# Channel gate over a 384x384x384 image on one core: a shorter lead load with the weight on the same queue, and the first tile gated in two parts

## Chip, cores, metric

One NeuronCore of one Trainium2 chip. The metric is the device time of one execution in microseconds. A run counts as slow here when it is over 1.5% above the fastest of its kernel.

## The reference

```python
def reference(x, w1d):                      # x: (1, 384, 384, 384) bf16, w1d: (1,) bf16
    g = jnp.einsum("bhwc->bc", x) / (H * W) # mean of each channel over all pixels
    s = _sigmoid(g * w1d[0])                # cut: with k = 1 the padding and loop come to this
    return x * s[:, None, None, :]
```

The gate is the sigmoid that multiplies x, one value for each channel. It needs the mean over the whole image before the first output element is known, so a plain kernel reads x twice. At 113.25 MB for one pass over x, that would be three passes of traffic.

## The kernel before

The kernel guesses. A "row" here is 128 pixels times 384 channels, 98,304 bytes. It computes a sigmoid (`s_early`) from the first 4 rows, gates and stores every tile with it while the true sums go on, and compares the bf16 result with the true sigmoid at the end. Only if they differ does a second pass run (it doesn't with these inputs). So x is read once and the output written once.

Data come in a lead of 12 rows and 19 tiles of 60 rows, in four slots of SBUF, the on-chip memory. DVE is the vector engine. A packet is one piece that a DMA engine moves, as the trace records it; a load or store lands when its end is signalled. Loads go to SyncE's queue; of the first three tiles half goes to ScalarE's queue, which later carries all stores. TensorE sums 52 rows of each tile with matmuls against ones, DVE sums the other 8 and does the gating. The weight (2 bytes) was queued on ScalarE behind half of the first tile:

```python
FIRST, EARLY, TILE, SLOTS, BOTH, OWN, PAUSE = 12, 4, 60, 4, 3, 8, 8
...
    load(base, FIRST, 0)                                     # lead: 12 rows, SyncE
    for k in range(BOTH):
        load(slot(k), TILE, row0(k), ("sync", "scalar"))     # halves of 30 rows
        if k == 0:
            plan.dma("scalar", w_one[0:1, 0:1], w1d.unsqueeze(0), writes=["w_one"])
    for k in range(BOTH, SLOTS):
        load(slot(k), TILE, row0(k))
    weight()                     # one matmul that spreads the weight; TensorE's first
    sum_first()                  # 3 matmuls over 4 rows
    ...                          # s_early on ScalarE
        def one(e, s):           # TensorE, each tile: 39 matmuls, one signal at their end
            e.wait_ge(ready, 1).then_inc(ready, -1)
            add_rows(e, 1, slot(s) * C, TILE - OWN, False, False).then_inc(
                plan.sems["tensor"], 1
            )
    ...
    def put(place, n, r0, to=None):          # gate in place on DVE, then store
        plan.op("vector", gate(to, place, n, s_early), ...)
        plan.final.append(
            plan.dma("scalar", dram(o_rows, r0, n), at(to, n), reads=rows(to, n))
        )
    ...
    for k in range(n_tiles):
        if k >= SLOTS:
            for i in ...:        # cut: which tiles are put here
                sum_own(i)       # DVE's 8 rows of tile i
                put(slot(i), TILE, row0(i))
            if k == SLOTS:
                pause(slot(k))   # ScalarE: waits for the first store, then 8 rows of dummy work
            load(slot(k), TILE, row0(k), ...)   # waits for the store that frees the slot
```

The gate overwrites the tile in place, so it must wait until TensorE has summed it.

## Time and profile before

528.62 us, median of the first 3 runs (528.31 to 529.32).

The lines below are of the page of the kernel before: the span, busy time by engine, and, in 40 slices of the span, DVE's busy tenths, the DMA engines' busy tenths and the GB/s moved; then the DMA queues (q1 is SyncE's, q10 ScalarE's) with packets, megabytes and share of 16 engines' span.

```profile
span 527.0 us, 1015 instructions
PE 198.5 (38%) x754; PEld 0.2 (0%) x2; DVE 353.9 (67%) x81; ACT 5.5 (1%) x5; POOL 0.3 (0%) x5
...
DVE  0639999649494858576666666666666666758892
...
DMA  9999999999999999999999999999999999999998
GB/s 383 434 421 418 448 448 395 444 448 448 395 444 448 448 395 444 448 444 399 444 448 444 399 444 448 445 399 444 444 444 406 441 444 444 406 441 444 444 406 363
...
q10 hardware_dynamic: 3314, 122.10, 53.6%
q1 hardware_dynamic: 2880, 104.40, 46.1%
...
HBM read 113.25 MB, written 113.25 MB: 430 GB/s over the span
```

53.6% and 46.1% are 99.7%: the DMA engines are busy the whole time. DVE is next with 67%. The slices of 395 and 448 GB/s are an effect of which whole packets fall into a slice; longer windows show the rate. The next lines are from the windows view of the kernel before: stretch, its length, busy time (count) of PE, PEld, DVE, ACT and POOL, then TensorE's clock, the DMA engines' busy share and GB/s.

```profile
0.00:10.00 10.00, 0.00 (x0) 0.00 (x0) 0.17 (x1) 1.49 (x2) 0.30 (x5) 1.00 0.93 376
10.00:44.00 34.00, 20.10 (x75) 0.20 (x2) 16.52 (x10) 0.61 (x1) 0.00 (x0) 1.00 1.00 430
50.00:56.00 6.00, 5.06 (x24) 0.00 (x0) 5.97 (x3) 0.00 (x0) 0.00 (x0) 1.00 1.00 369
100.00:480.00 380.00, 143.99 (x546) 0.00 (x0) 249.30 (x43) 0.00 (x0) 0.00 (x0) 0.69 1.00 434
```

From 10 to 44 us there are only loads (430 GB/s), from 100 to 480 us loads and stores (434 GB/s). Two stretches are lower: the first 10 us and the 6 us around the first store.

The timeline of the kernel before, early stage (start, duration, engine, line, what; in brackets the engine's idle time before it and what ended it):

```profile
15.31 0.16 PE L409 MATMUL w_all<-w_one,ones 1*128 1x1 bf16 x1 [15.31 <-DMA w_one<-in_w1d_dram]
...
19.63 0.61 ACT L440 ACTIVATE s_early<-total,w_scaled 128x384 bf16<-128x384 f32 x1 [15.80 <-DVE total L315]
...
24.18 11.17 PE L244 MATMUL acc<-arena,ones 128*128 128x512 bf16 x39 [6.04 <-PEq L283]
35.45 12.16 DVE L207 TENSOR_TENSOR arena<-arena,s_early 128x23040 bf16<-128x23040 bf16 x1 [10.63 <-PE acc L244]
...
47.64 18.36 ACTq L109 DMA_DIRECT2D out_dram<-arena  x2
```

TensorE waits 15.31 us for the weight, the early sigmoid runs at 19.63, the first tile's sums start at 24.18 when its SyncE half has landed, DVE waits 10.63 us for the 39 matmuls, and the first store is issued at 47.64. The end, from the chain of waits of the kernel before (start, duration, what):

```profile
403.47 47.25 DMA out_dram<-arena
...
450.74 38.79 DMA arena<-in_x_dram
...
489.55 12.16 DVE arena L207
```

This chain names the things that ended last, but a link of it can be covered by queued DMA work. At 489.5 to 501.7 us, for example, DVE gates the last tile while the DMA engines still work off earlier stores.

### The profile page before, as it was taken

To read this page: it belongs to the slowest core of one execution; us is meant where nothing else is said; L and a number is where in the kernel's file an instruction comes from. 1 tells how busy PE (TensorE), PEld (TensorE's weight loads), DVE (VectorE), ACT (ScalarE), POOL (GpSimd) and SP (SyncE) were. 2 spreads that over 40 slices of the span, in tenths; PEclk is the share of its full clock that TensorE was granted. 3 is DMA by queue.
4 is the path that set the end of the run, shared out by engine and by line. 5 is a ranking of instruction groups with operands and counts; after the bars stand their busy time and mean duration, and the time that the engine had idled before them with its cause. 6 is when DMAs were issued, how large, how long until landed. Compare 5 with 4: busy or idle time off the path is not lost. (4 is left out here: it accounts for less than half of the span.)

```text
span 527.0 us, 1015 instructions
## 1 busy us (share of the span) xinstructions
PE 198.5 (38%) x754; PEld 0.2 (0%) x2; DVE 353.9 (67%) x81; ACT 5.5 (1%) x5; POOL 0.3 (0%) x5
## 2 busy tenths in 40 slices
PE   0389170070706151524333342516060707070810
PEld 0000000000000000000000000000000000000000
DVE  0639999649494858576666666666666666758892
ACT  1000020000000000000000000000000000000000
POOL 0000000000000000000000000000000000000000
PEclk9999766576767667675758585858585858585765
DMA  9999999999999999999999999999999999999998
GB/s 383 434 421 418 448 448 395 444 448 448 395 444 448 448 395 444 448 444 399 444 448 444 399 444 448 445 399 444 444 444 406 441 444 444 406 441 444 444 406 363
DMA packets 6196, 226.51 MB, mean 430 GB/s; under 512 B 690, under 2 KB 690, under 8 KB 690
## 3 DMA queue, kind: packets, MB, share of 16 engines
q10 hardware_dynamic: 3314, 122.10, 53.6%
q1 hardware_dynamic: 2880, 104.40, 46.1%
q14 instruction: 2, 0.02, 0.0%
HBM read 113.25 MB, written 113.25 MB: 430 GB/s over the span
## 5 line engine op out<-in xcount | busy, mean ns | idle before, releaser
L244 PE MATMUL acc<-arena,ones 128*128 128x512 bf16 x749 | 196.6, 429 | 288.4 <-PEq L283 288.4
L207 DVE TENSOR_TENSOR arena<-arena,s_early 128x23040 bf16<-128x23040 bf16 (+1 forms) x20 | 233.5, 11677 | 78.0 <-PE acc L244 73.6
L327 DVE TENSOR_REDUCE part<-arena 128x384 f32<-128x3072 bf16 x18 | 96.4, 5355 | 67.3 <-DMA arena<-in_x_dram 67.3
L334 DVE TENSOR_TENSOR own<-own,part 128x384 f32<-128x384 f32 x18 | 10.0, 558 | 0.6
L418 DVE TENSOR_SCALAR w_scaled<-w_all 128x1 f32<-128x1 f32 x2 | 0.2, 152 | 14.3 <-PE w_all L409 14.3
L409 PE MATMUL w_all<-w_one,ones 1*128 1x1 bf16 x1 | 0.2, 158 | 15.3 <-DMA w_one<-in_w1d_dram 15.3
L244 PE MATMUL acc_own<-terms,ones 128*128 128x384 bf16 x3 | 1.4, 479 | 10.5 <-DVE terms L345 10.5
L327 DVE TENSOR_REDUCE own<-arena 128x384 f32<-128x3072 bf16 x1 | 5.3, 5305 | 0.0
L474 ACT ACTIVATE arena<-total,w_scaled 128x384 bf16<-128x384 f32 x1 | 0.6, 615 | 439.0 <-DVE total L315 439.0
L315 DVE TENSOR_TENSOR total<-total,acc 128x128 f32<-128x128 f32 (+2 forms) x11 | 4.5, 408 | 0.4
L392 ACT ACTIVATE arena<-warm 128x3072 bf16<-128x3072 f32 x1 | 2.8, 2763 | 54.1 <-DMA out_dram<-arena 54.1
L313 DVE COPY total<-acc 128x384 f32<-128x384 f32 x1 | 0.6, 558 | 1.2 <-PE acc L244 1.2
L403 ACT ACT_TABLE_LOAD x1 | 1.3, 1283 | 2.3 <-issue 2.3
L352 DVE TENSOR_TENSOR own<-own,terms 128x384 f32<-128x384 f32 x2 | 1.1, 558 | 0.1
L345 DVE CAST terms<-own 128x384 bf16<-128x384 f32 x3 | 1.1, 357 | 0.1
L482 DVE TENSOR_TENSOR total<-arena,s_early 128x384 f32<-128x384 uint16 x1 | 0.6, 557 | 0.7 <-ACT arena L474 0.7
L370 DVE TENSOR_TENSOR total<-total,acc_own 128x384 f32<-128x384 f32 x1 | 0.6, 554 | 0.6 <-PE acc_own L244 0.6
L426 DVE MEMSET ones<- 128x128 bf16 x1 | 0.2, 165 | 1.0 <-PEq L596 1.0
L440 ACT ACTIVATE s_early<-total,w_scaled 128x384 bf16<-128x384 f32 x1 | 0.6, 615 | 15.8 <-DVE total L315 15.8
L242 PE MATMUL acc<-arena,ones 128*128 128x512 bf16 x1 | 0.6, 608 | 0.0
L490 DVE TENSOR_REDUCE wrong<-total 128x1 f32<-128x384 f32 x1 | 0.6, 552 | 0.0
L403 ACT ACTIVATE warm<-warm 128x1 f32<-128x1 f32 x1 | 0.2, 203 | 0.0
(8 smaller groups left out, 0.9 us busy)
## 6 DMA issues: line engine op xcount, KB each, us to landing
out_dram<-arena ACTq DMA_DIRECT2D x19, 5760.0 KB, 47.4
arena<-in_x_dram SPq DMA_DIRECT2D x16, 5760.0 KB, 38.9
arena<-in_x_dram ACTq DMA_DIRECT2D x3, 2880.0 KB, 27.4
arena<-in_x_dram SPq DMA_DIRECT2D x3, 2880.0 KB, 36.4
arena<-in_x_dram SPq DMA_DIRECT2D x1, 1152.0 KB, 10.3
out_dram<-arena ACTq DMA_DIRECT2D x1, 1152.0 KB, 16.9
w_one<-in_w1d_dram ACTq DMA_DIRECT2D x1, 0.0 KB
```

Source lines behind the costliest of these rows:

```text
L207: return lambda e: e.tensor_tensor(to_v, v, s_b, ALU.mult)
L242: loaded.append(e.matmul(bank, weights, moving, start=start, stop=stop))
L244: return e.add_instruction(mybir.InstMatmult(name=nc.get_next_instruction_name(), engine=mybir.EngineType.PE, ins=[e.lower_ap(moving), e.l ...
L313: emit = lambda e, part=part, of=of: e.tensor_copy(part, of)
L315: emit = lambda e, part=part, of=of: e.tensor_tensor(part, part, of, ALU.add)
L327: lambda e: e.reduce_sum(to[:], view, axis=mybir.AxisListType.X),
L334: lambda e: e.tensor_tensor(own[:], own[:], part[:], ALU.add),
L345: lambda e, term=term: e.tensor_copy(term, own[:]),
L352: lambda e, term=term: e.tensor_tensor(own[:], own[:], term, ALU.subtract),
L370: lambda e: e.tensor_tensor(total[:], total[:], acc_own[:, :C], ALU.add),
L392: lambda e: e.activation(to, warm[:, 0:1].broadcast_to([P, PAUSE * C]), ACT_F.Sigmoid),
L403: lambda e: e.activation(warm[:, 1:2], warm[:, 0:1], ACT_F.Sigmoid),
```

## The change

Its intent: get the early sigmoid, the first gate and so the first store sooner. The lead shrinks to 8 rows with the weight right behind it on SyncE; the other 4 rows go to ScalarE's queue behind its half of the first tile; TensorE signals after 32 of the 52 rows of a tile, and the first tile is gated in parts of 32 and 28 rows; the pause becomes 9 rows instead of 8.

```diff
-FIRST, EARLY, TILE, SLOTS, BOTH, OWN, PAUSE = 12, 4, 60, 4, 3, 8, 8
+FIRST, EARLY, TILE, SLOTS, BOTH, FORE, OWN = 12, 4, 60, 4, 3, 32, 8
+PAUSE = 9
@@ sum_others, one tile @@
-            add_rows(e, 1, slot(s) * C, TILE - OWN, False, False).then_inc(
-                plan.sems["tensor"], 1
-            )
+            for r, n in ((0, FORE), (FORE, TILE - OWN - FORE)):
+                add_rows(e, 1, (slot(s) + r) * C, n, False, False).then_inc(
+                    plan.sems["tensor"], 1
+                )
@@ put: one gate for each part, one store for all @@
-        plan.op("vector", gate(to, place, n, s_early), ...)
+        for m in parts or [n]:
+            plan.op("vector", gate(to + i, place + i, m, s_early), ...)
+            i += m
@@ order of the loads @@
-    load(base, FIRST, 0)
-    for k in range(BOTH):
-        load(slot(k), TILE, row0(k), ("sync", "scalar"))
+    LEAD = EARLY + 4
+    load(base, FIRST, 0, hi=LEAD)
+    plan.dma("sync", w_one[0:1, 0:1], w1d.unsqueeze(0), writes=["w_one"])
+    for k in range(SLOTS):
+        load(slot(k), TILE, row0(k), ("sync", "scalar") if k < BOTH else ("sync",))
         if k == 0:
-            plan.dma("scalar", w_one[0:1, 0:1], w1d.unsqueeze(0), writes=["w_one"])
-    for k in range(BOTH, SLOTS):
-        load(slot(k), TILE, row0(k))
+            load(base, FIRST, 0, ("scalar",), lo=LEAD)
@@ main loop @@
-                put(slot(i), TILE, row0(i))
+                put(slot(i), TILE, row0(i), parts=None if i else (FORE, TILE - FORE))
... (cut: the bounds lo and hi of load(), the signals that go with the two parts, and that two DMAs
     instead of one are issued on SyncE ahead of the start)
```

## The prediction

> What bounds the kernel now. It reads 113.25 MB and writes 113.25 MB. The page's queue table gives the two queues 53.6% and 46.1% of 16 engines' span: 99.7% busy. The windows view gives a DMA share of 1.00 and 434 GB/s between 100 and 480 us; DVE has 67% of the span, PE 38%. In the packet records a 46080-byte packet takes 1.702 us, load or store: 433 GB/s on 16 engines, so 226.5 MB need 523 of the 527.0 us. The Trainium skill ("DMA: Bandwidth & Descriptors", "Specifications") gives a fabric ceiling of 435 GB/s; the trace agrees.
>
> Only some 4 us are not pure moving. By the packet records: about 1.1 us before the first packet, about 1 of slow first packets, about 0.9 at 51 to 54 us, where the last load packets before the first store packet take 2.3 to 2.7 us instead of 1.7, and about 1 at the end.
>
> What the change does. (a) The lead load shrinks from 12 to 8 rows, the weight right behind it. Now the lead lands at 10.3 us but the weight, queued behind 30 rows, at 15.2, and TensorE waits for it (waits view: 15.3 us). Laying the packets out anew with measured durations (0.86 us for 23040 bytes), I estimate the lead at 6.5 and the weight at 8 us, so the early sigmoid at 13 instead of 19.6. (b) SyncE's half of the first tile lands at about 17.5 instead of 24.1. (c) The first gate waits for 24 matmuls (6.9 us) instead of 39 (11.2 us); its parts cost 6.5 + 5.7 us, as much as the single 12.16. Estimated first store issue: 37 us instead of 47.6; the second 55 instead of 65.5. (d) The longer pause costs 0.35 us once (now 2.76).
>
> How much lies on the critical path. Almost none. The chain of waits names DVE and PE pieces, but DMA has queued work during all of them. An earlier store only mixes stores into time in which loads ran at the same rate; both queues share the same engines (same page, "Issuing engines are not separate DMA queues"; the trace shows their packets alternating, and the same 433 GB/s with one queue or two). At the end the last tile's store (issued 501.7) waits 8.8 us behind the previous one (landing 510.5), so the last gate isn't critical either. What can be won is the 0.9 us at the first store, if it now queues behind load packets on ScalarE's queue (whose last early load lands at 42.7 now, about 44 then). Against it: smaller packets, under 0.1 us.
>
> Predicted: 528.1 us, 8 times in 10 between 527.2 and 529.2. Faster by over 2%: 0.5%; within 2%: 97.5%; slower by over 2%: 2%.
>
> What would show the steps. First matmul at 8 us; early sigmoid near 13; two first gates of 6.5 and 5.7 us; first store issue at 35 to 39 us; queue shares still adding to over 99%; 433 to 434 GB/s in mid-span; fewer slow packets at the first store, or moved to 45 us.
>
> What would make it wrong. If the new phase of loads against stores lets both queues run dry together, each gap adds its length. If the early sigmoid differed from the true one, the second pass would nearly double the time; the same four rows are summed, so I don't expect it. If mixed traffic ran faster than loads alone, the earlier store would pay; the records show no difference above 1%.

## The result, and the profile after

528.22 us median of 6 runs (528.09 to 529.50) against 529.16 (528.31 to 530.30) of 6 runs of the kernel before: the ratio is 0.9986, with a 95% interval of 0.9971 to 1.0001. It is the same time within 2%, and the interval just reaches no change. A ratio is the mean time of one kernel's fast runs over that of the other's of the same rounds, so it isn't quite the ratio of the medians quoted.

The page of the changed kernel, same lines as before:

```profile
span 526.6 us, 1019 instructions
PE 212.1 (40%) x754; PEld 0.2 (0%) x2; DVE 354.2 (67%) x82; ACT 5.8 (1%) x5; POOL 0.3 (0%) x5
...
DVE  1498999249484857666666756666667675849892
...
DMA  9999999999999999999999999999999999999998
GB/s 380 436 424 453 413 448 406 434 448 445 406 438 448 441 410 438 448 434 413 441 448 424 420 445 445 424 424 441 448 424 420 445 445 427 420 445 445 427 420 370
...
q10 hardware_dynamic: 3456, 122.49, 53.8%
q1 hardware_dynamic: 2882, 104.01, 45.9%
...
HBM read 113.25 MB, written 113.25 MB: 430 GB/s over the span
```

The same bytes, 99.7% again, and a span 0.4 us shorter. The windows view of the changed kernel:

```profile
0.00:10.00 10.00, 0.61 (x3) 0.20 (x2) 0.39 (x3) 1.49 (x2) 0.30 (x5) 1.00 0.92 371
10.00:44.00 34.00, 20.97 (x70) 0.00 (x0) 25.05 (x10) 0.61 (x1) 0.00 (x0) 0.90 1.01 434
50.00:56.00 6.00, 2.53 (x7) 0.00 (x0) 6.00 (x1) 0.00 (x0) 0.00 (x0) 0.61 1.03 403
100.00:480.00 380.00, 152.30 (x546) 0.00 (x0) 247.08 (x42) 0.00 (x0) 0.00 (x0) 0.69 1.00 434
```

Up to 44 us and from 100 to 480 us the rates are those of before within some 1%; in the 6 us around the first store it is 403 GB/s instead of 369. The early timeline of the changed kernel:

```profile
9.39 0.16 PE L415 MATMUL w_all<-w_one,ones 1*128 1x1 bf16 x1 [9.39 <-DMA w_one<-in_w1d_dram]
...
13.71 0.61 ACT L446 ACTIVATE s_early<-total,w_scaled 128x384 bf16<-128x384 f32 x1 [9.33 <-DVE total L319]
...
18.79 11.12 PE L247 MATMUL acc<-arena,ones 128*128 128x512 bf16 x39 [6.57 <-PEq L286]
26.79 12.23 DVE L209 TENSOR_TENSOR arena<-arena,s_early 128x12288 bf16<-128x12288 bf16 x2 [6.77 <-PE acc L247]
...
39.05 20.77 ACTq L109 DMA_DIRECT2D out_dram<-arena  x2
```

Every early step is sooner: TensorE starts at 9.39 us instead of 15.31, the early sigmoid runs at 13.71 instead of 19.63, the first gate starts at 26.79 instead of 35.45 and the first store is issued at 39.05 instead of 47.64. Yet the last load is waited for until the same moment, by the chain of waits of the changed kernel:

```profile
404.24 44.59 DMA out_dram<-arena
...
448.85 40.77 DMA arena<-in_x_dram
...
489.64 12.16 DVE arena L209
```

489.64 against 489.55: 8.6 us gained at the first store are gone. Where? The table gives times from the first load's issue, worked out from the issue, landing and packet records of the traces (us; one profiled execution of each kernel, the experiments of the next section with it). "4th load" is the one of the fourth tile, the last that waits for nothing.

```
                 first store:              ScalarE's last   4th load   second store
kernel           issue  1st packet landed  early load lands lands      lands
before           47.64    53.12    74.29      42.61          69.19       96.38
after            39.05    50.94    74.17      53.33          70.33       94.51
lead_only        41.51    51.16    74.43      53.14          70.85       94.75
split_only       44.60    48.80    73.53      42.57          71.82       93.99
wait_3           47.98    53.21    74.45      53.16          69.35       94.80
four_wait        48.08    53.03    74.41      36.16          69.29       94.73
four_on_sync     43.07    47.45    77.01      36.09          76.83       99.44
wait_6           64.34    65.21    79.38      53.27          60.09      107.33
```

In the six kernels above the last two, the first store is issued between 39 and 48 us and lands between 73.5 and 74.5. The reason is the sum of bytes. By then the engines must have moved 252 rows of loads and 60 rows of store, 312 x 98,304 bytes = 30.67 MB, which at 433 GB/s takes 70.8 us; in the kernel before, 1.1 us without packets at the start and 1.6 us of slow packets make up most of the rest (the changed kernel has 1.1 and 1.1). An earlier store only takes engine time away from the fourth load, which lands that much later; the pair is done at the same time.

Second, the earlier issue hardly gives an earlier start: 8.6 us at the issue are 2.2 us at the first packet. The change itself put ScalarE's early loads back from 42.6 to 53.3 us, and the store stands in that queue behind them. An empty queue doesn't make a store start at once either: in the kernel before, ScalarE's last early packet ended at 41.3 us and the store issued at 47.64 still had its first packet only 5.5 us later; with ScalarE's queue empty it is 4.2 to 5.0 us in split_only, four_on_sync and four_wait, while SyncE's load runs, and 0.9 us in wait_6, where the engines were idle.

The span splits further by the packet records. Engine time without a packet is 1.76 us of the span before and 1.56 after; packets slower than the usual time of their size cost 1.70 us before and 1.42 after. The two differences sum to 0.48, which covers the 0.4 us. But this is one profile of each; a second profile of the changed kernel (after_again) has a span of 526.8 us, which leaves half of the difference.

### The profile page after: what moved, and what is told of

The parts are those of the page before. It is cut to its first block, busy times and chain, and to the rows that moved or that the text cites. A ratio compares the mean times of both kernels' runs of the same rounds, so it can differ in the third digit from the quotient of the medians.

```text
span 526.6 us, 1019 instructions
## 1 busy us (share of the span) xinstructions
PE 212.1 (40%) x754; PEld 0.2 (0%) x2; DVE 354.2 (67%) x82; ACT 5.8 (1%) x5; POOL 0.3 (0%) x5
## 5 line engine op out<-in xcount | busy, mean ns | idle before, releaser
L247 PE MATMUL acc<-arena,ones 128*128 128x512 bf16 x749 | 210.2, 451 | 281.5 <-PEq L286 281.5
L209 DVE TENSOR_TENSOR arena<-arena,s_early 128x23040 bf16<-128x23040 bf16 (+3 forms) x21 | 233.6, 11129 | 84.3 <-PE acc L247 80.6
L398 ACT ACTIVATE arena<-warm 128x3456 bf16<-128x3456 f32 x1 | 3.1, 3082 | 59.9 <-DMA out_dram<-arena 59.9
L245 PE MATMUL acc<-arena,ones 128*128 128x512 bf16 x1 | 0.6, 610 | 0.0
```

Of the source, the lines that this page charges most:

```text
L209: return lambda e: e.tensor_tensor(to_v, v, s_b, ALU.mult)
L245: loaded.append(e.matmul(bank, weights, moving, start=start, stop=stop))
L247: return e.add_instruction(mybir.InstMatmult(name=nc.get_next_instruction_name(), engine=mybir.EngineType.PE, ins=[e.lower_ap(moving), e.l ...
L398: lambda e: e.activation(to, warm[:, 0:1].broadcast_to([P, PAUSE * C]), ACT_F.Sigmoid),
```

## The experiments

Twelve kernels ran, in three groups of four; those of one group ran on one chip beside the kernel before. All gave the right result except fewer_bytes.

### after_again: the changed kernel once more

No edit.

> The changed kernel once more, to be compared with the others of this call on the same chip. Theory (moving bytes bounds the time; the first store's issue time is off the critical path): 0.1% to 0.3% under before, 527.8 to 528.8 us; packets of the load before the first store slowed for about 0.6 us in sum. Rival (the earlier first store itself pays): the same time, so this run doesn't tell them apart; it is the yardstick.

Measured: 528.54 us median of 6 (527.92 to 529.17); before 528.54 median of 11 (528.24 to 531.74); ratio 0.9987, interval 0.9960 to 1.0013. So the change gains about 0.1% by both measurements, and neither interval tells it from none. Over its 12 runs in two groups the changed kernel never went over 529.5.

### lead_only: the new load order without the two-part gate

```diff
-            for r, n in ((0, FORE), (FORE, TILE - OWN - FORE)):
-                add_rows(e, 1, (slot(s) + r) * C, n, False, False).then_inc(
+            add_rows(e, 1, slot(s) * C, TILE - OWN, False, False).then_inc(
...
-                put(slot(i), TILE, row0(i), parts=None if i else (FORE, TILE - FORE))
+                put(slot(i), TILE, row0(i))
```

> The new load order without the gate in two parts. The first gate waits for all 39 matmuls, so the first store is issued at about 42 us instead of 39. Theory: its packets still stand behind ScalarE's last early load, which lands at 53.4 us, so the store lands at 74.2 +- 0.3 us as before and the time equals that of the changed kernel within 0.3 us. Rival (an earlier first store pays one to one): 3 us over the changed kernel.

Measured: 528.18 us (528.04 to 528.67), 0.36 under after_again. The store was issued 2.5 us later than in the changed kernel (41.51), had its first packet 0.2 us later and landed 0.3 us later. The two-part gate gains nothing; its rival, 3 us slower, is out.

### split_only: the two-part gate without the new load order

The edit is the `FORE` parts of the change's diff, on the kernel before, with `PAUSE = 8`.

> The gate in two parts alone, old load order. First store issued at about 43.3 us instead of 47.6. ScalarE's queue is empty from 42.2 us there, so unlike in the changed kernel this store should start early: first packet at 46 to 49 us instead of 53.2, landing at 67 to 70 us instead of 74.3. Theory: total within 0.8 us of before all the same, 527.8 to 529.3. Rival (earlier store pays one to one): 4 us under before.

Measured: a miss. The first packet came at 48.80 as expected, but the store landed at 73.53, not 67 to 70: I had forgotten that the fourth load shares the engines till 71.8 us. The time was 533.72 us median of 7 (528.79 to 534.43), ratio 1.0082, interval 1.0055 to 1.0110. One run, the profiled one, was 528.79; the other six were 532.9 to 534.4. With the earlier start of the first store six runs of seven were 5 us slower, not 4 us faster; but the only profile is of the good run, which has the earlier start too, so it doesn't show why. The next experiment caught a slow case in a trace, of another kernel.

### four_on_sync: the 4 left-over rows on SyncE's queue

```diff
-            load(base, FIRST, 0, ("scalar",), lo=LEAD)
+            load(base, FIRST, 0, ("sync",), lo=LEAD)
```

> The changed kernel with the 4 left-over rows on SyncE's queue instead of ScalarE's. Theory of the queues (they alternate packet by packet, so 8 packets of 3072 bytes per engine hold ScalarE's queue up for 8 packets of 23040, some 6.8 us): ScalarE's last early load lands at 42 to 46 us instead of 53.4, the first store's first packet comes at 44 to 48 us instead of 51.0 and it lands at 66 to 70 us instead of 74.2, with its issue still at about 39. Theory of the time: total as the changed kernel within 0.6 us. Rival (earlier store pays): 5 us under it.

Measured: the theory of the queues held for ScalarE's loads and was even too timid: the last early one lands at 36.09 us instead of 53.1 to 53.3. Two expectations missed: the first store is issued at 43.07 and not at about 39, as SyncE's half of the first tile now lands at 22.9 instead of 18.6, and it lands at 77.0 and not at 66 to 70. The small packets are what moves ScalarE's loads. The Trainium skill ("DMA: Bandwidth & Descriptors", "Queues, rings and completion order") says that each engine "round-robins between the queue rows it has work for, at *packet* granularity". This trace agrees: while both queues have work, their packets alternate one by one whatever their size (in the changed kernel, 128 packets of 3072 bytes on ScalarE's queue beside 134 of 23040 on SyncE's from 13.2 to 21.1 us), so 8 packets of 3072 bytes an engine (0.12 us each) wait for 8 of 23040 (0.86 us each), and the queue that carries the small ones falls behind by about 7 us and the other gets ahead.

The time, though, missed both expectations: 533.83 us (532.28 to 535.68), ratio 1.0092, interval 1.0059 to 1.0126. The windows view of four_on_sync:

```profile
45.00:51.00 6.00, 6.00 (x29) 0.00 (x0) 4.07 (x3) 0.00 (x0) 0.00 (x0) 1.00 1.02 407
51.00:72.00 21.00, 8.13 (x37) 0.00 (x0) 20.97 (x4) 0.00 (x0) 0.00 (x0) 0.76 0.99 386
72.00:90.00 18.00, 11.14 (x38) 0.00 (x0) 16.47 (x4) 3.08 (x1) 0.00 (x0) 0.71 1.01 399
100.00:480.00 380.00, 152.68 (x536) 0.00 (x0) 242.57 (x43) 0.00 (x0) 0.00 (x0) 0.69 1.00 433
```

The engines are not idle (0.99 of 51 to 72 us) but move only 386 GB/s there. By the packet records, the 96 store packets that began between 51 and 73 us took 2.03 us on average, 60 of them over 1.9 (typically 2.2), where the store packets of the kernels before and after took 1.70 between 55 and 72 us, none of them over 1.9; the loads beside the slow ones took 1.73. Over the whole span slow packets cost some 3.7 us more than in the changed kernel (5.09 against 1.42): 2.1 of the 5.09 from 51 to 73 us and 1.7 from 73 to 100 us, where loads are slow too. Another 0.9 us is lost without packets, most of it in the last 8 us. My new theory: this first store goes through its tile in step with the fourth load (they land 0.2 us apart, by the table), while in the kernels before and after it trails by 5.1 and 3.8 us; in step is slow. (The 77.35 and 77.54 in the next expectation are these two landings, read some 0.5 us later than in the table.)

### four_wait: four_on_sync with the first store delayed

```diff
                 sum_own(i)
+                if i == 0:
+                    for _ in range(3):
+                        idle(i)          # reduce_sum of 8 rows into a spare tile, on DVE
```

> four_on_sync (533.8 us) with three spare reductions of 5.36 us on DVE ahead of the first gate, so the first store is issued at about 48.2 us instead of 43.1. Phase theory (a store and a load that go through their tiles in step, packet for packet, slow the store's packets from 1.70 to about 2.2 us; in four_on_sync the fourth load lands at 77.35 and the first store at 77.54): the later store trails the load by some 4 packets again, landing about 5 us after it, so the time falls back to 527.8 to 529.3 us, that is, 5 us of delay make it 5 us faster. Rival 1 (an earlier first store pays): 5 us slower than four_on_sync, 539. Rival 2 (the 4 rows on SyncE's queue cost it): stays at 533 to 535.

Measured: 528.46 us (528.22 to 529.02). Adding 16 us of useless DVE work, which delays the first store by 5.0 us (48.08 instead of 43.07), went with a time 5.4 us shorter. The two ran on different chips, but the kernel before took 528.54 and 528.62 on them. The windows view of four_wait, from 51 us:

```profile
51.00:72.00 21.00, 10.05 (x42) 0.00 (x0) 20.93 (x6) 0.00 (x0) 0.00 (x0) 0.80 0.93 402
72.00:90.00 18.00, 8.27 (x34) 0.00 (x0) 17.97 (x4) 3.08 (x1) 0.00 (x0) 0.78 1.01 435
```

The windows' edges blur the rate (402 GB/s at a DMA share of 0.93, after 495 in the window before). In the packet records the load and store packets between 55 and 72 us take 1.70 us again, none over 1.9. So the slow stretch depends on when the first stores start (the second is 3 us later too), and the place of the 4 rows alone doesn't make it. That "in step" is the reason isn't shown by this yet.

### pause_1 and pause_long: moving the fifth load against the stores

pause_1 shortens the pause, pause_long runs it four times.

```diff
-PAUSE = 9
+PAUSE = 1                                # pause_1

+        for _ in range(4):               # pause_long
             plan.op("scalar", lambda e: e.activation(...), ...)
```

> The changed kernel with a pause of 1 row instead of 9, so the fifth load is issued some 2.7 us earlier. Phase theory: the fifth load then trails the second store by about 11 us instead of 13.7, in a period of 27.2, still far from in step: 527.8 to 529 us, as the changed kernel. If the length of the pause matters by itself, 2.7 us less or more than it.

> The changed kernel with the pause four times over (12.3 us instead of 3.1), so the fifth load is issued at about 86.6 us, when the second store (alone till then) has ended and the third starts at about 88: loads and stores in step from there. Phase theory: store packets of 2.2 us and about 385 to 410 GB/s as long as the step holds, so 535 to 575 us, by how long it holds. Rival (the slow stretch in four_on_sync belongs to the start of the stores alone): both queues are never dry, so 528 to 529.5.

Measured, pause_1: a miss, and in two groups: 528.34 and 528.64, and four runs of 531.55 to 533.09; median 531.72, ratio 1.0036, interval 1.0000 to 1.0072. The profile fell on the 528.34 run and shows nothing slow.

Measured, pause_long: 530.21 us (529.34 to 530.39), ratio 1.0008, interval 0.9969 to 1.0047. The phase theory expected 535 to 575. In its trace a load and a store land 1.8 us apart (142.5 and 140.7 us after the first issue), and the packets that ran beside each other between 115 and 141 us took 1.70 us, none over 1.9. So being nearly in step isn't enough to slow them: the theory falls as I had put it. Its span is 2.0 us over that of the changed kernel: 1.35 us more time without packets and 0.65 of slow packets. Its last load lands 7 us later (496.56), so the last store is issued later too.

What stays: with another length of the pause (pause_1, pause_long) or another start of the first store (four_on_sync, split_only) some or all executions are 2 to 6 us longer. What decides it within one kernel, and what makes the store packets slow, is open. No run changes the pause from 8 to 9 rows alone, so what that part of the change does is open too. The 20 runs of lead_only, wait_3, vector_more and four_wait, all with 9 rows, have none over 530 us, but all 6 of four_on_sync, with 9 rows too, are over 532.

### wait_3 and wait_6: how late the first store may be

The edit is that of four_wait on the changed kernel, with 3 and 6 reductions.

> The changed kernel with three spare reductions of 5.36 us on DVE ahead of the first gate (6.8 us of them fall into a wait that is there anyway), so the first store is issued at about 48.4 us instead of 39.05, later than in the kernel before. Theory: free; the store's packets still come after ScalarE's last early load (53.4 us), it lands at 74 to 75 us, and the time equals that of the changed kernel within 0.6 us. Rival (issue of the first store on the critical path): +9.3 us, 537.5.

> Six spare reductions, first store issued at about 64.4 us (+25.4). Theory: the early loads alone (252 rows, 24.8 MB at 433 GB/s) end at about 59 us, so from there to about 66 us the DMA engines are dry, and again for about 4 us after the first store lands, because the second store and the fifth load are both late: +9 to +13 us, 537 to 541. Rival (one to one): +25, 553. This shows where the slack ends.

Measured, wait_3: 528.35 us (528.01 to 529.92). The first store is issued 8.9 us later, at 47.98, later than in the kernel before the change; it lands 0.3 us later and nothing is lost. This undoes all that the change won at the issue, at no cost. From the timeline of wait_3, the two gates and then the issue of the first store:

```profile
35.74 12.21 DVE L209 TENSOR_TENSOR arena<-arena,s_early 128x12288 bf16<-128x12288 bf16 x2
...
47.98 0.36 ACTq L109 DMA_DIRECT2D out_dram<-arena  x1
```

Measured, wait_6: 542.95 us (541.59 to 544.58), 2 us over the range; ratio to the kernel before 1.0239, interval 1.0173 to 1.0305, so slower, but not clearly by 2%. The windows view of wait_6:

```profile
60.00:65.00 5.00, 5.00 (x25) 0.00 (x0) 5.00 (x2) 0.00 (x0) 0.00 (x0) 1.00 0.00 0
79.00:84.00 5.00, 0.00 (x0) 0.00 (x0) 5.00 (x2) 1.27 (x1) 0.00 (x0) 0.50 0.35 147
100.00:480.00 380.00, 140.81 (x510) 0.00 (x0) 254.25 (x44) 0.00 (x0) 0.00 (x0) 0.68 1.00 433
535.00:543.00 8.00, 0.00 (x0) 0.00 (x0) 0.00 (x0) 0.00 (x0) 0.00 (x0) 0.50 0.26 108
```

The early loads end at 60.1 us, and until 65.2 nothing moves; then again from 79.4 to about 84. That is the cost that was expected. The excess over the range lies where I hadn't looked: at the end, where the engines' packets run out (108 GB/s in the last 8 us, 5.4 us of them without packets against 1.3 in the changed kernel), and in slow packets after the gaps (3.4 us against 1.4). Once the queues run dry, the first store does count; the kernel before, whose first store packet came at 53.1 us, was 7 us away from that.

### vector_more: DVE work in every tile

```diff
                 sum_own(i)
+                idle(i)                  # 5.36 us more of DVE, 18 tiles
```

> The changed kernel with one spare reduction of 5.36 us ahead of the gate of each of the first 18 tiles: +96 us of DVE, 67% to 85% of the span. Theory: DVE has 9 us of slack in each 27.2 us period and stores are queued 14 to 18 us ahead, so the time stays within 0.6 us of the changed kernel. Rival (the chain of waits with DVE's gates and reductions bounds it): at least the DVE share of that chain more, tens of us.

Measured: 528.55 us (528.22 to 528.88). The busy line of the page of vector_more:

```profile
PE 216.5 (41%) x754; PEld 0.2 (0%) x2; DVE 450.4 (86%) x100; ACT 5.8 (1%) x5; POOL 0.3 (0%) x5
```

96 us more of DVE, 86% of the span, and no time lost. So neither DVE nor the chain that names it bounds the kernel.

### bytes_more and fewer_bytes: the bytes themselves

bytes_more adds 14 loads of 8 rows into spare memory on SyncE's queue. fewer_bytes stores 56 rows of each 60 (wrong result).

```diff
+            if k > SLOTS:                # bytes_more
+                plan.final.append(plan.dma("sync", at(base + FIRST + 1, 8),
+                    dram(x_rows, row0(k), 8), reads=["pause"], writes=["spare"]))

-            plan.dma("scalar", dram(o_rows, r0, n), at(to, n), reads=rows(to, n))
+            plan.dma("scalar", dram(o_rows, r0, n)[:, : (n - n // 15) * C],
+                at(to, n - n // 15), reads=rows(to, n))       # fewer_bytes
```

> The changed kernel with 14 extra loads of 8 rows (11.0 MB) in mid-run into spare memory, never used; the result stays right. Theory: each byte costs its time at 433 GB/s: +25.4 us, with 6144-byte packets at 234 ns +26.2, so 553.5 to 555.5. Rival (DVE, PE or the chain of waits bounds it): less than half of that.

> WRONG RESULT ON PURPOSE: of each 60-row tile only 56 rows are stored (packets of 43008 instead of 46080 bytes); waits, loads and all compute stay. Theory (moved bytes bound the time): 7.47 MB less at 433 GB/s is 17.2 us less than the changed kernel, 510 to 512 us. Rival (DVE, PE or the loads alone bound it): less than half of that.

Measured, bytes_more: 570.52 us, median of 4 (564.42 to 577.51, the last one slow), 42 us more, where 25 to 26 were expected. The experiment is confounded by my edit: each spare load overwrites the last, so SyncE's queue waited for it, 375 us in all by the queue's waits (in the changed kernel it waits 367 us, but for stores). The loads came late, and after the first store ScalarE's queue ran dry eight times, for 3.6 to 19 us each. Its profile (577.51) is also slow. The time grew by more than the bytes' own; how much of it is the bytes can't be told, so nothing is taken from this run.

Measured, fewer_bytes: 511.28 us (511.16 to 512.56), ratio to the kernel before 0.9662, interval 0.9624 to 0.9700. From the changed kernel's 528.22 to 528.54 that is 16.9 to 17.3 us less for 7.47 MB, 17.2 us at 433 GB/s. The bytes line of its page, to compare with the same line of the changed kernel above:

```profile
HBM read 113.25 MB, written 105.78 MB: 430 GB/s over the span
```

The same 430 GB/s over a shorter span: the time follows the bytes, with DVE, TensorE, waits and loads as they were.

## Why the prediction was right

- **The time.** Predicted 528.1 (527.2 to 529.2), measured 528.22, within 2% as 97.5% of the chance said. That the two agree to 0.1 us is luck: the forecast gain came from the 0.9 us at the first store, which wasn't won (below), and the measured gain can't be told from none. The reason given for no change, though, held. It was that moved bytes bound the time. vector_more (96 us of DVE for nothing) and wait_3 (the first store 8.9 us later for nothing) rule the rivals out, and fewer_bytes gives the slope, 17 us for 7.47 MB. The Trainium skill ("DMA: Bandwidth & Descriptors", "Specifications") puts the fabric ceiling at 435 GB/s; the traces have 433 to 434 in mid-span, so nothing but fewer bytes is left to win there.
- **Early steps.** Right in kind, each too hopeful. The lead landed at 7.8 us (predicted 6.5) and the weight at 9.3 (8): I left out that the lead lands 1.2 to 1.3 us after its last packet ends (before: last packet ends at 9.0, landing 10.3; after: 6.6 and 7.8). The sigmoid ran at 13.7 (13), SyncE's half of the first tile landed at 18.6 (17.5). The first 24 matmuls took 8.0 us (6.9): I had taken 24/39 of the 11.2 us, but in both traces the first dozen matmuls of the first tile start 0.43 us apart and the later ones 0.22. The first store was issued at 39.05, just outside 35 to 39, the second at 59.5 instead of 55. The gate's parts took 6.56 and 5.75 us (6.5 and 5.7), the longer pause cost 0.32 (0.35).
- **The term that was mis-sized** is "ScalarE's queue (whose last early load lands at 42.7 now, about 44 then)". It landed at 53.3. I shared the bandwidth out by bytes; the queues alternate by packets, and the 4 rows put eight 0.12 us packets per engine into ScalarE's queue, each of which waits for a 0.86 us packet, and later its 23040-byte packets alternate with SyncE's 46080-byte ones. four_on_sync, with the small packets on the other queue, moved the landing to 36.1. It also made the second tile, and so the second store, later than predicted.
- **"What can be won is the 0.9 us at the first store".** Not won. The slow packets before the first store cost 14.1 engine-us of the 16 engines before (0.9 us), and 9.1 and 11.2 in the two profiles of the changed kernel (0.6 and 0.7 us), but 14.4 in lead_only and 15.0 in wait_3, where the store also stood behind loads in its queue. So an empty queue ahead of the store isn't their cause. split_only has no such packets at its first store and some at 93 us instead.
- **What I didn't foresee.** "If the new phase of loads against stores lets both queues run dry together" was the only harm that I named. Near this design an edit to the order of the loads or to the first store's start can cost 5 us with the DMA engines still 99% busy: four_on_sync and, most of the time, split_only. The changed kernel stayed clear of it in its 12 runs. It may even do so better than the kernel before: 9 of that one's 35 runs are over 530 us and none of the changed kernel's 12. With equal chances, 12 clean runs would come up in about 3 of 100 (0.74 to the 12th power), so this is a hint, and no trace shows a long run of the kernel before.

No version that ran beats the changed kernel clear of noise; lead_only (528.18) equals it with less code.

## What to carry to other kernels

When the queues add up to 99% of the DMA engines and the rate sits at the ceiling, and as long as they do not run dry (as in wait_6), starting something earlier only changes which bytes go first; test it by delaying the same thing on purpose, which is easier than speeding it up. Share two queues' time by packets and not by bytes: a small load in a queue beside big packets puts everything behind it back (ScalarE's last early load landed at 53.3 us instead of 36.1 here). And judge a kernel near such a limit by many runs: a median near 528.5 can hide a tail of runs 2 to 5 us longer, and small edits to a pause or to the first store's start made that tail the rule.

## What the Trainium skill lacked or had wrong

- "DMA: Bandwidth & Descriptors", "Issuing engines are not separate DMA queues": it says that using several engines will only save the sequencer's time to initiate. For the order of landing this says too little: the queue that 4 rows (0.39 MB) were put on moved the landing of ScalarE's last early load from 53.3 to 36.1 us. The whole time went from 528.5 to 533.8 with it, but not by the queue alone: with the first store delayed as well it was 528.46. The rule of alternation in "Queues, rings and completion order" explains the landing, but the page doesn't draw the conclusion that a queue's share goes with its packet size.
- No page tells of the slow stretch of four_on_sync: 60 of 96 store packets took about 2.2 us instead of 1.70 beside loads, with the DMA engines busy throughout. The cause is open.
- The same page, "Where 436 GB/s comes from", says that for transfers between HBM and SBUF the HBM side (about 358 GB/s) binds. With one core at work this kernel had 434 GB/s over 380 us, loads and stores mixed, which is the fabric figure. "HBM Reference" ("Specifications (TRN2)") has it nearer, with about 425 for a core alone.
- No page has it that store packets can take 2.2 us instead of 1.70 while all engines are busy, for a stretch of 20 us, depending on when the first store starts beside a load (four_on_sync against four_wait). The cause is open.
